# Both norms of an attention and gated feed-forward kernel: ScalarE's reciprocal square root with one Newton step in place of a root and a reciprocal

## The chip, the cores and the metric

The kernel runs on one core of one Trainium2 chip. The metric is the device time of one execution in microseconds (us), given as the median of several runs. The engines are named as in the profile: PE is TensorE (matmuls), PEld its weight loads, DVE is VectorE, ACT is ScalarE, POOL is GpSimd and SP is SyncE, which issues most DMAs.

## The reference

For each of 8 batches there is an attention without a softmax over 8 heads of 64 columns and 576 positions, followed by a root-mean-square norm, and then a gated feed-forward layer whose one half is normalised over its columns and mixed over positions:

```python
kv = np.einsum('bhsd,bhse->bhde', k, v)
out = np.einsum('bhsd,bhde->bhse', q, kv)
rms = np.sqrt(np.mean(out * out, axis=-1, keepdims=True) + 1e-06)
x = out / rms * g_norm                    # per head, then heads side by side: (8, 576, 512)
h = np.maximum(x @ w_in, 0.0)             # d_ff = 1024
u, v = h[..., :512], h[..., 512:]
v_n = (v - mean(v)) / np.sqrt(var(v) + 1e-06)
v_s = np.einsum('ts,bsd->btd', w_spatial, v_n) + b_spatial[None, :, None]
return (u * v_s) @ w_out
```

All is float32. Both norms need 1/sqrt(mean + 1e-6): the first one value for each position and head, the second one value for each position.

## The kernel before

**Tiles.** A batch has 576 positions: four blocks of 128 and a tail of 64. The tails of two batches, an even one and the odd one behind it, are worked on together as a fifth block of 128. The eight heads go as four pairs.

**Attention.** For each pair TensorE makes k'v (L162, tile pskv), ScalarE and VectorE copy the two diagonal blocks to KVB or KVO (L179, L180), and TensorE multiplies by q (L237, pso). The four blocks of 128 positions of a pair stand side by side in one PSUM bank of 512 columns, 8 groups of 64. `norm_a` squares them: either one ScalarE instruction (L223) and a VectorE sum (L224), or eight ScalarE instructions of 64 columns that sum as they go (L220). The sums are ss, 128 x 8. `rsqrt_a` and `rsqrt_b` make 1/sqrt of ss/64 + 1e-6, and `norm_b` multiplies the bank by it (L229, tile x). TensorE transposes x (L265, pstr), and ScalarE and VectorE split the result into a high part XH (L258) and the remainder XL (L259).

**Products in float32.** After the first batch every product of float32 matrices is three passes of the faster format fp32r: high by high, high by low and low by high (`three`, `hl`, `split`; L353 is the high part on ScalarE, L354 the remainder on VectorE). Batch 0 uses plain float32 matmuls while weights are still being decoded and split.

**Feed-forward.** hv (L350, psh) is the half that is normalised: ScalarE empties the bank with a Relu (L323), VectorE makes mean and variance (L329, L330, tile mv), `rsqrt` follows, and the values are normalised either on VectorE (L333) or by one VectorE operation that makes the bias (L336) and one ScalarE instruction (L337). The u half and the mixing over positions are made by a scheme of seven products of half-size blocks instead of eight (L566; banks psua, psub, psuc and psa, psb, psc); VectorE and ScalarE empty and add up their parts (L519 to L549 for U, L615 to L636 and L586, L588 for the gate). In batch 1 u is made without that scheme (`u_unit`, L317 with tile psu, emptied by L453). The last product (L317 with WO) gives the output, which ScalarE copies out (L668). Weights arrive as 64-bit numbers: L713 on ScalarE and L719 to L723 on VectorE decode them; `make_out` does so for the four slabs of w_out, and `split_out` then splits a slab into WO and stores a copy (spare_o, L748). `load_out` loads a slab (L688, tile stage).

**Counts.** There are 40 norms of heads (tile names end in h) and 36 of the feed-forward half (names end in v). The norms of the tails are among both.

**Order.** The text of PLAN, between [ and ], pins the first part of the program (the attention of batch 0 and its first products, some 45 us) for PE, ACT and SP in the order written. FIRST, EVEN, ODD, SEVEN and GATED give the order in which later steps are written down, but there the tile framework's list scheduler (`schedule_with_timeline_sim=True`) puts the instructions of each engine in an order by its own estimate of their times. Each engine then works through its queue in that order and waits at the first instruction that is not ready. All products but the attention's use a pool of four PSUM banks (ps_mm) in turn, so a product starts when the bank of the fourth product before it is empty.

**The lines that the change touches** are `rsqrt_a` and `rsqrt_b`, which both norms call, and the warming instruction L813, whose function decides which table ScalarE loads first.

Of the kernel before, what the change touches and what calls it, by code (L numbers as in the profile page):

```python
# [8 lines left out]
F32 = mybir.dt.float32  # L9
# [3 lines left out]
AF = mybir.ActivationFunctionType  # L13
ALU = mybir.AluOpType
# [5 lines left out]
P = 128  # L20
# [10 lines left out]
EPS = 1e-6  # L31
# [42 lines left out]
def body(ctx: ExitStack, tc, qT, kvm, kvt, g2, w_in, wsT, bsp, w_out, out):  # L74
    nc = tc.nc
# [6 lines left out]
    small = ctx.enter_context(tc.tile_pool(name="small", bufs=2))  # L82
# [46 lines left out]
    epsc = edge.tile([P, 8], F32, name="epsc", tag="epsc")[:, 0:1]  # L129
# [62 lines left out]
    def rsqrt(ss, n, rows, mul, tag):  # L192

        return rsqrt_b(*rsqrt_a(ss, n, rows, mul, tag))

    def rsqrt_a(ss, n, rows, mul, tag):
        a, s0, q, r = (small.tile([P, n], F32, name=f"{x}{tag}", tag=f"{x}{tag}")[0:rows]
                       for x in "asqr")
        nc.scalar.activation(s0, ss, AF.Sqrt, bias=epsc[0:rows], scale=mul)
        nc.vector.tensor_scalar(a, ss, mul, EPS, op0=ALU.mult, op1=ALU.add)  # L200
        nc.vector.reciprocal(q, a)
        return s0, q, r

    def rsqrt_b(s0, q, r):

        nc.vector.tensor_tensor(r, s0, q, op=ALU.mult)
        nc.vector.scalar_tensor_tensor(q, s0, -0.5, r, op0=ALU.mult, op1=ALU.mult)
        nc.vector.scalar_tensor_tensor(r, q, 1.5, r, op0=ALU.add, op1=ALU.mult)
        return r

    def heads(ap):
# [2 lines left out]
    def norm_a(ps, rows=P, accumulate=False):  # L214
        x = work.tile([P, 512], F32, name="x", tag="x")[0:rows]
        ss = small.tile([P, 8], F32, name="ss", tag="ss")[0:rows]
        if accumulate:
            for h in range(8):
                cols = slice(h * D, (h + 1) * D)
                nc.scalar.activation(x[:, cols], ps[0:rows, cols], AF.Square,  # L220
                                     accum_out=ss[:, h:h + 1])
        else:
            nc.scalar.activation(x, ps[0:rows], AF.Square)  # L223
            nc.vector.tensor_reduce(ss, heads(x), axis=AX.X, op=ALU.add)  # L224
        return ps, x, rows, rsqrt_a(ss, 8, rows, 1.0 / D, "h")

    def norm_b(ps, x, rows, parts):
        r = rsqrt_b(*parts)
        nc.vector.tensor_tensor(heads(x), heads(ps[0:rows]),  # L229
                                r.unsqueeze(2).broadcast_to([rows, 8, D]), op=ALU.mult)  # L230
        return x
# [578 lines left out]

    nc.vector.memset(KVB[:, 1], 0.0)
    nc.vector.memset(epsc, EPS)
    nc.scalar.activation(small.tile([P, 1], F32, name="warm", tag="av"), epsc, AF.Sqrt)  # L813
    nc.gpsimd.memset(KVB[:, 0], 0.0)
    for kt in KT:
        nc.gpsimd.memset(kt[TAIL:P], 0.0)
# [223 lines left out]
```

## Time and profile before

| what | value |
|---|---|
| median of 3 runs | 513.03 us (511.57 to 513.43) |
| span of the profiled execution | 511.2 us |
| from the span to the three runs | 0.4 to 2.2 us more |
| PE busy | 498.9 us (98%), 3436 matmuls |
| PE weight loads busy | 438.4 us (86%) |
| DVE busy | 408.8 us (80%), 1193 instructions |
| ACT busy | 292.8 us (57%), 1000 instructions |
| granted TensorE clock | 1.00 |

The profile is of one execution. A row of a group of instructions gives the line, the engine, the operation, what it writes and reads, and how often; busy time is the union of their durations. "A <- B: t" in the list of waits says that A's engine stood idle for t in total until B released it. Times in a timeline count from the start of the span. The device time of the profiled execution itself is not listed; the runs beside it bound it.

### The profile page before, as it was taken

What the parts mean: (1) busy time and instruction counts of PE and PEld (TensorE: products, weight loads), DVE (VectorE), ACT (ScalarE), POOL (GpSimd) and SP (SyncE); (2) the same over time, 40 slices, a digit from 0 to 9 for tenths busy, and PEclk for the clock granted to TensorE, in tenths of its full rate; (3) what the DMA queues carried; (4) which work ended last, traced back from release to release, by engine and by line L of the source; (5) the groups of instructions that cost most, each with busy time, mean ns of one, the idle gap of its engine ahead of it and who ended that gap; (6) DMA issues with size and microseconds to landing.
All of it is one profiled execution on the core that took longest, in us unless ns stands there. A gap on an engine that the chain in (4) does not pass through costs nothing.

```text
span 511.2 us, 9846 instructions
## 1 busy us (share of the span) xinstructions
PE 498.9 (98%) x3436; PEld 438.4 (86%) x3436; DVE 408.8 (80%) x1193; ACT 292.8 (57%) x1000; POOL 28.7 (6%) x58
## 2 busy tenths in 40 slices
PE   6999999999999999999999999999999999999996
PEld 6758788898888899989998899988998889988995
DVE  3898599688997889778795689878898589987870
ACT  2555456896734796456641689347742579536421
POOL 5000000000010300010000100010000100010000
PEclk9999999999999999999999999999999999999999
DMA  7995300635354435354426615324444512315213
GB/s 256 311 347 193 103 23 2 238 90 174 123 193 137 129 126 207 117 170 138 133 93 228 203 41 194 112 78 176 135 165 144 171 30 63 131 42 165 91 76 103
DMA packets 28293, 72.22 MB, mean 141 GB/s; under 512 B 3602, under 2 KB 8210, under 8 KB 26708
## 3 DMA queue, kind: packets, MB, share of 16 engines
q1 hardware_dynamic: 23412, 48.01, 28.6%
q0 software_dynamic: 4832, 23.60, 13.9%
q8 instruction: 27, 0.44, 0.4%
q14 instruction: 22, 0.18, 0.1%
HBM read 58.48 MB, written 13.11 MB: 140 GB/s over the span
## 4 chain that ended last, share of the span: by engine, by line
PE 78%; DVE 8%; ACT 7%; DMA 5%; issue 1%; SPq 0%; ACTq 0%; DVEq 0%
PE pso L317 15%; PE psh L350 12%; PE psb L566 7%; PE pso L237 4%; PE psc L566 4%; PE psa L566 4%; PE psub L566 4%; PE pskv L162 4%; PE psu L428 3%; PE psa L437 3%; PE psua L566 3%; PE psh L404 3%; PE psuc L566 2%; PE pstr L265 2%; DMA KV<-kvm 2%; ACT x L220 2%
## 5 line engine op out<-in xcount | busy, mean ns | idle before, releaser
L317 PE MATMUL pso<-WO,G 128*128 128x512 f32 x384 | 94.4, 397 | 0.0
L317 PEld LDWEIGHTS pso<-WO,G 128*128 128x128 f32 x384 | 70.6, 188 | 14.5
L353 ACT CAST G<-SUMg 128x288 fp32r<-128x288 f32 (+1 forms) x56 | 22.8, 406 | 44.6 <-DVE SUMg L588 44.4
L220 ACT ACTIVATE x<-pso 128x64 f32<-128x64 f32 x208 | 44.8, 254 | 5.7 <-PE pso L237 5.5
L220 ACT ACTIVATION_READ_ACCUMULATOR x<-pso 128x1 f32 x208 | 43.9, 240 | 0.0
L350 PE MATMUL psh<-WVL,XH 128*128 128x512 f32 x112 | 43.9, 392 | 0.0
L350 PE MATMUL psh<-WVH,XH 128*128 128x512 f32 x112 | 43.8, 396 | 0.0
L350 PE MATMUL psh<-WVH,XL 128*128 128x512 f32 x112 | 43.3, 391 | 0.0
L668 ACT COPY o<-pso 128x512 f32<-128x512 f32 x35 | 20.2, 594 | 38.9 <-PE pso L317 28.7
L354 DVE TENSOR_TENSOR VL<-v,VH 128x512 fp32r<-128x512 f32 (+1 forms) x56 | 34.6, 620 | 2.7 <-ACT VH L353 2.2
L353 ACT CAST VH<-v 128x512 fp32r<-128x512 f32 (+1 forms) x56 | 31.7, 574 | 3.3 <-DVE v L382 2.1
L337 ACT ACTIVATE v<-v,mv,rv 128x512 f32<-128x512 f32 x28 | 23.5, 840 | 10.6 <-DVE mv L336 10.5
L354 DVE TENSOR_TENSOR G<-SUMg,G 128x288 fp32r<-128x288 f32 (+1 forms) x56 | 23.4, 417 | 7.2 <-ACT G L353 6.9
L258 ACT ACTIVATE XH<-pstr,gcol 128x512 fp32r<-128x512 f32 x28 | 19.4, 700 | 11.4 <-PE pstr L265 11.2
L566 PE MATMUL psb<-WSH,VH 128*128 128x288 f32 x84 | 25.6, 305 | 0.3 <-DVE U L549 0.2
L329 DVE BATCH_NORM_STATS2 s<-v 128x6 f32<-128x512 f32 x32 | 21.9, 689 | 4.5 <-ACT v L323 3.9
L350 PEld LDWEIGHTS psh<-WVH,XH 128*128 128x128 f32 x112 | 21.0, 188 | 4.6 <-ACT o L668 0.2
L350 PEld LDWEIGHTS psh<-WVL,XH 128*128 128x128 f32 x112 | 21.1, 188 | 4.4
L566 PE MATMUL psb<-WSL,VH 128*128 128x288 f32 x84 | 24.8, 295 | 0.0
L350 PEld LDWEIGHTS psh<-WVH,XL 128*128 128x128 f32 x112 | 21.0, 188 | 4.3
L162 PEld LDWEIGHTS pskv<-KV 128*64 128x64 f32 x512 | 18.1, 140 | 7.8 <-issue 3.9
L566 PE MATMUL psb<-WSH,VL 128*128 128x288 f32 x84 | 24.6, 295 | 0.0
(244 smaller groups left out, 1419.4 us busy)
## 6 DMA issues: line engine op xcount, KB each, us to landing
KV<-kvm SPq DMA_DIRECT2D x31, 512.0 KB, 5.0
WO<-spare_o POOLq DMA_DIRECT2D x12, 1024.0 KB, 7.0
UX<-spare_u POOLq DMA_DIRECT2D x18, 512.0 KB, 5.7
out<-o SPq DMA_DIRECT2D x32, 256.0 KB, 2.6
qt<-qT SPq DMA_DIRECT2D x16, 288.0 KB, 3.5
stage<-w_in SPq DMA_DIRECT2D x8, 512.0 KB, 6.5
qt<-qT SPq DMA_DIRECT2D x16, 256.0 KB, 2.7
KT<-kvt SPq DMA_DIRECT2D x32, 64.0 KB, 4.8
```

Of the source, the lines that this page charges most:

```text
L162: return nc.tensor.matmul(ps[h:h + D, at:at + D], of[:, 0, h:h + D], of[:, 1, h:h + D], start=c == 0, stop=c == NC)
L220: nc.scalar.activation(x[:, cols], ps[0:rows, cols], AF.Square, accum_out=ss[:, h:h + 1])
L237: nc.tensor.matmul(ps[:, c * P:(c + 1) * P], qt[:, c * P:(c + 1) * P], st[p], start=True, stop=True)
L258: nc.scalar.activation(hi, ps, AF.Copy, scale=gcol)
L317: nc.tensor.matmul(ps, lt, rh, start=i == 0, stop=i == n - 1)
L329: nc.vector.bn_stats(s6, v)
L337: nc.scalar.activation(v, v, AF.Identity, bias=m, scale=r)
L350: nc.tensor.matmul(ps, lt, rh, start=k == 0 and i == 0, stop=k == NP - 1 and i == 2)
L353: nc.scalar.copy(hi, x)
L354: nc.vector.tensor_tensor(lo, x, f32(hi), op=ALU.subtract)
L566: nc.tensor.matmul(ps, lt, rh, start=start and i == 0, stop=stop and i == len(pairs) - 1, skip_group_check=True)
L668: nc.scalar.copy(o, ps)
```

## The change

Before, ScalarE makes s0, the square root of a = ss * mul + EPS, while VectorE makes a once more and its reciprocal q. Then r = s0 * q is a first value of 1/sqrt(a), and two more VectorE operations improve it: q = -0.5 * s0 * r, r = (q + 1.5) * r. Now ScalarE makes the first value y of 1/sqrt(a) itself, and three VectorE operations are one Newton step on it: r = -0.5 * mul * y * y, r = (ss + EPS/mul) * r, which is -0.5 * a * y * y, and r = (r + 1.5) * y. The VectorE operations go from five to three for each norm. The sums ss (or the variance in mv) are now read by VectorE behind ScalarE's instruction instead of beside it.

```diff
     def rsqrt_a(ss, n, rows, mul, tag):
-        a, s0, q, r = (small.tile([P, n], F32, name=f"{x}{tag}", tag=f"{x}{tag}")[0:rows]
-                       for x in "asqr")
-        nc.scalar.activation(s0, ss, AF.Sqrt, bias=epsc[0:rows], scale=mul)
-        nc.vector.tensor_scalar(a, ss, mul, EPS, op0=ALU.mult, op1=ALU.add)
-        nc.vector.reciprocal(q, a)
-        return s0, q, r
-
-    def rsqrt_b(s0, q, r):
-
-        nc.vector.tensor_tensor(r, s0, q, op=ALU.mult)
-        nc.vector.scalar_tensor_tensor(q, s0, -0.5, r, op0=ALU.mult, op1=ALU.mult)
-        nc.vector.scalar_tensor_tensor(r, q, 1.5, r, op0=ALU.add, op1=ALU.mult)
+        y, r = (small.tile([P, n], F32, name=f"{x}{tag}", tag=f"{x}{tag}")[0:rows] for x in "yr")
+        nc.scalar.activation(y, ss, AF.Abs_reciprocal_sqrt, bias=epsc[0:rows], scale=mul)
+        return ss, y, r, mul
+
+    def rsqrt_b(ss, y, r, mul):
+
+        nc.vector.scalar_tensor_tensor(r, y, -0.5 * mul, y, op0=ALU.mult, op1=ALU.mult)
+        nc.vector.scalar_tensor_tensor(r, ss, EPS / mul, r, op0=ALU.add, op1=ALU.mult)
+        nc.vector.scalar_tensor_tensor(r, r, 1.5, y, op0=ALU.add, op1=ALU.mult)
         return r
...
-    nc.scalar.activation(small.tile([P, 1], F32, name="warm", tag="av"), epsc, AF.Sqrt)
+    nc.scalar.activation(small.tile([P, 1], F32, name="warm", tag="yv"), epsc, AF.Abs_reciprocal_sqrt)
```

From L209 on every line's number is 3 less in the changed program (L323 becomes L320, L713 becomes L710). ScalarE's order has one load of a function table in either program, ahead of the warming instruction.

The scheduler's order changes too, outside the pinned part. Three places follow. The first is ScalarE's queue behind the pinned part, in batch 1. WTL and WTH are the tail of the mixing weights, v is the Relu that empties psh, G is the gate of batch 0, and t is the first step of the decoding of a slab of w_out. Before:

```order
L787 CAST WTL_88<-WTL_87 64x576
L180 COPY KVB<-pskv 64x2x64
L789 CAST WTL_88<-WTL_87 1x576
L323 ACTIVATE v<-psh 128x512 x2
L789 CAST WTL_88<-WTL_87 1x576
L353 CAST G<-U 128x512
L353 CAST GT<-U 128x64
```

Some rows further down, behind the other three casts of G, the same queue goes on before the change:

```order
L323 ACTIVATE v<-psh 128x512
L220 ACTIVATE x,ss<-pso 128x64 x2
L199 ACTIVATE sv<-mv,epsc 128x1
L713 ACTIVATE t<-stage 128x512
L199 ACTIVATE sv<-mv,epsc 128x1
```

The same place of ScalarE's queue after the change:

```order
L784 CAST WTL_88<-WTL_87 64x576
L180 COPY KVB<-pskv 64x2x64
L786 CAST WTL_88<-WTL_87 1x576
L710 ACTIVATE t<-stage 128x512
L320 ACTIVATE v<-psh 128x512 x2
L786 CAST WTL_88<-WTL_87 1x576
L350 CAST G<-U 128x512
```

The decoding step t stands ahead of the two Relus that empty psh, where it stood behind the third Relu.

The second place is SyncE's queue of DMAs at about the same time. spare_o are the stored copies of split slabs, stage is the load of the next slab, KV and KT are keys and values of a later pair. Before:

```order
L748 DMA spare_o<-WO 128x512 x3
L142 DMA KV_105<-kvm 128x1024
L748 DMA spare_o<-WO 128x512
L688 DMA stage<-w_out 128x1024
L142 DMA KV_104<-kvm 128x1024
```

After the change:

```order
L745 DMA spare_o<-WO 128x512 x4
L685 DMA stage<-w_out 128x1024
L142 DMA KV_105<-kvm 128x1024
L142 DMA KV_104<-kvm 128x1024
L143 DMA KT_106<-kvt 64x256
```

The load of the slab moves ahead of one load of keys and values.

The third place is VectorE's queue in batch 4, where the seven products of u end (300 to 320 us of the span before). U is added up from psub and psuc, v is the normalised half of the tails, SUMg its difference of halves, and names in v and h are norms. Before:

```order
L336 SCALAR_TENSOR_TENSOR mv<-mv,rv 128x1
L538 TENSOR_TENSOR U<-psub,U 128x288
L201 RECIPROCAL qh<-ah 128x8
L206 TENSOR_TENSOR rv<-sv,qv 128x1
L207 SCALAR_TENSOR_TENSOR qv<-sv,rv 128x1
L208 SCALAR_TENSOR_TENSOR rv<-qv,rv 128x1
L333 TENSOR_SCALAR v<-v,mv,rv 128x512
L206 TENSOR_TENSOR rh<-sh,qh 128x8
L529 TENSOR_TENSOR U<-psub,U 128x288
L393 TENSOR_TENSOR SUMg<-v 128x256
L207 SCALAR_TENSOR_TENSOR qh<-sh,rh 128x8
L544 TENSOR_TENSOR U<-psub,U 128x288
```

After the change:

```order
L333 SCALAR_TENSOR_TENSOR mv<-mv,rv 128x1
L535 TENSOR_TENSOR U<-psub,U 128x288
L203 SCALAR_TENSOR_TENSOR rv<-yv 128x1
L204 SCALAR_TENSOR_TENSOR rv<-mv,rv 128x1
L205 SCALAR_TENSOR_TENSOR rv<-rv,yv 128x1
L330 TENSOR_SCALAR v<-v,mv,rv 128x512
L526 TENSOR_TENSOR U<-psub,U 128x288
L203 SCALAR_TENSOR_TENSOR rh<-yh 128x8
L390 TENSOR_TENSOR SUMg<-v 128x256
L541 TENSOR_TENSOR U<-psub,U 128x288
```

The additions to U keep their order, and the operations of the norms between them are fewer.

## The prediction

> **What bounds the kernel now.** I read the page first (busy time of each engine), then a table of stretches, then the list of waits for TensorE, and last the timeline at the places where the new order differs. The page's first part:
>
> ```profile
> PE 498.9 (98%) x3436; PEld 438.4 (86%) x3436; DVE 408.8 (80%) x1193; ACT 292.8 (57%) x1000; POOL 28.7 (6%) x58
> ```
>
> TensorE is busy for 498.9 of 511.2 us. The change takes work from VectorE, which is busy for 80%. So the question is how much TensorE waits for VectorE. The table of stretches (from and to, length, then busy us of PE, PEld, DVE, ACT and POOL with instruction counts, clock, DMA share, GB/s) places TensorE's 12.3 us of idle time:
>
> ```profile
> 0.00:24.00 24.00, 18.87 (x158) 15.76 (x159) 14.07 (x37) 8.89 (x21) 7.43 (x20) 1.00 0.88 281
> 24.00:504.00 480.00, 476.84 (x3267) 420.32 (x3266) 394.28 (x1156) 282.68 (x977) 21.27 (x38) 1.00 0.41 134
> 504.00:512.00 8.00, 3.20 (x14) 2.28 (x13) 0.42 (x1) 1.18 (x3) 0.00 (x0) 0.94 0.49 164
> 88.00:150.00 62.00, 60.67 (x486) 54.10 (x486) 53.61 (x160) 44.92 (x151) 2.68 (x4) 1.00 0.47 157
> 190.00:210.00 20.00, 19.59 (x178) 18.81 (x177) 18.88 (x53) 12.61 (x57) 1.06 (x2) 1.00 0.45 153
> 300.00:320.00 20.00, 19.26 (x146) 18.50 (x146) 19.14 (x63) 18.34 (x94) 1.06 (x2) 1.00 0.48 158
> 420.00:440.00 20.00, 19.60 (x152) 19.16 (x151) 18.73 (x63) 18.15 (x93) 1.06 (x2) 1.00 0.39 132
> 456.00:464.00 8.00, 8.00 (x37) 6.48 (x36) 5.73 (x12) 5.50 (x11) 1.59 (x3) 1.00 0.67 200
> ```
>
> Idle are 5.1 us in the first 24 us (VectorE has 14 of 24 us of work there, the DMA engines are 0.88 busy) and 4.0 us after the last matmul (511.2 - 504 - 3.20), where VectorE has one copy left. Between 24 and 504 only 480 - 476.84 = 3.16 us are idle, and four stretches hold nearly all of it: 1.33, 0.41, 0.74 and 0.40 us. In the last three VectorE is full (18.7 to 19.1 of 20 us). A busy row can hide a little, since a matmul's end is drawn after its successor's start; the weight loads show the same waits longer. TensorE's waits from 24 to 504 us, first as matmuls, then the same as weight loads (total, times, longest):
>
> ```profile
> PE pstr L265 <- DVE x L229: 0.4, 2, 0.3
> ...
> PE psa L566 <- DVE U L549: 0.3, 1, 0.3
> PE psb L566 <- DVE U L549: 0.2, 1, 0.2
> PE psa L566 <- DVE U L544: 0.2, 1, 0.2
> ...
> PEld psb L566 <- DVE U L549: 0.8, 2, 0.5
> PEld psa L566 <- DVE U L549: 0.6, 1, 0.6
> PEld psa L566 <- DVE U L544: 0.5, 1, 0.5
> ```
>
> The three waits for L549 and L544 are 0.7 us as matmuls and 1.9 as loads; the normalised tile (L229) is waited for twice, 0.4 us. I take twice the idle time as the real loss: some 6 us between 24 and 504, of which ScalarE or VectorE decide nearly all. That is the ceiling of what a faster norm can give: 1.2%.
>
> A rule speaks against this reading. The Trainium skill, "Perfetto Trace Analysis", section Identifying the Most-Contended Engine, says that matmul busy time is no good measure of TensorE's headroom and that weight-load busy time and MFU are. By it 14% of the span, some 72 us, would be open. The trace does not agree: in 456 to 464 the loads are busy 6.48 of 8 us (81%) while 37 matmuls follow one another every 0.22 us with no wait; 81% is what a full TensorE looks like with 512 columns.
>
> **The change part by part.** Instructions by line (count, least/median/greatest ns):
>
> ```profile
> L199 ACT ACTIVATE sh<-ss,epsc x40: 287/302/437, 12.9 to 438.3; 128x8 f32<-128x8 f32 x40
> ...
> L200 DVE TENSOR_SCALAR ah<-ss x40: 159/166/173, 12.9 to 439.3; 128x8 f32<-128x8 f32 x40
> L200 DVE TENSOR_SCALAR av<-mv x36: 131/153/155, 43.4 to 476.2; 128x1 f32<-128x1 f32 x36
> L201 DVE RECIPROCAL qh<-ah x40: 191/196/204, 13.1 to 440.1; 128x8 f32<-128x8 f32 x40
> L201 DVE RECIPROCAL qv<-av x36: 109/164/166, 44.9 to 476.4; 128x1 f32<-128x1 f32 x36
> ...
> L208 DVE SCALAR_TENSOR_TENSOR rh<-qh,rh x40: 147/159/170, 14.1 to 441.5; 128x8 f32<-128x8 f32 x40
> ```
>
> From the list of waits, the timeline (start, length) and the chain:
>
> ```profile
> DVE rv L206 <- ACT sv L199: 3.0, 6, 0.6
> ...
> 110.24 0.14 DVE L200 TENSOR_SCALAR av<-mv 128x1 f32<-128x1 f32 x1
> 110.30 0.16 DVE L200 TENSOR_SCALAR ah<-ss 128x8 f32<-128x8 f32 x1
> 110.42 0.17 DVE L201 RECIPROCAL qv<-av 128x1 f32<-128x1 f32 x1
> ...
> 290.39 0.17 DVE av L200
> ...
> 290.84 0.17 DVE rv L206
> ```
>
> Removed are L200 and L201 in 76 norms. At full durations: 40 x (166+196) + 36 x (153+164) ns = 25.9 us. Packed behind other work one costs only the distance to the next start, 0.06 to 0.12 us (110.24, 110.30, 110.42): 152 x 0.09 = 13.7 us. So VectorE loses 14 to 26 us of 408.8. The three operations left are of L208's kind and count; L206 to L208 were three as well, so they cost nothing new. The ScalarE instruction keeps its shape, bias and scale; a different function I price as the same row, 0.29 to 0.44 us, change 0.
>
> Latency gains less. From L200 to L206 it is 0.45 us in the row of 290.39, but the ScalarE root ran beside them for 0.3 us plus two hand-overs, and this stays; a lone norm gets 0.1 us shorter (an estimate: 0.45 less 0.3 and the hand-overs), one that waits for ScalarE (the six waits of 3.0 us) not at all: VectorE then stands at its first operation instead of its third.
>
> A scheduler orders everything outside the hand-written start by its own estimates, so less VectorE work also shuffles the program; the rows in the section on the change show it. Priced by stretch:
>
> - 0 to 24 and after 504: nothing. No norm releases TensorE there.
> - 24 to 88: nothing; TensorE is full.
> - The ends of the first products in batches 2, 4 and 6 (190, 300, 420): idle 0.41 + 0.74 + 0.40 = 1.55, by loads 3.1 us. In the second of them five norms end on VectorE (L208 in that stretch: busy, count):
>
> ```profile
> 300.00:320.00 20.00, 0.80 (x5) 1.00 0.48 158
> ```
>
>   So 10 operations leave, 0.9 us packed and 1.7 at full length, out of the queue that holds the L544 and L549 that TensorE waits for. But ScalarE is as full (18.34, 18.15 of 20), and the hidden half may stay. Ends: 0 and -3.1; I take half, **-1.5**.
> - 88 to 150: here an order change costs. The decode of the third slab of the output weights (L713 on ScalarE) stood behind the four casts of G; now it stands ahead of the two L323 that empty PSUM. Rows of ScalarE, SyncE and TensorE:
>
> ```profile
> 98.18 0.67 ACT L789 CAST WTL<-WTL 1x576 fp32r<-1x576 f32 x1
> 98.87 1.09 ACT L323 ACTIVATE v<-psh 128x512 f32<-128x512 f32 x2
> ...
> 103.36 0.59 ACT L323 ACTIVATE v<-psh 128x512 f32<-128x512 f32 x1
> ...
> 104.42 0.67 ACT L713 ACTIVATE t<-stage 128x512 f32<-128x512 f32 x1
> ...
> 94.46 0.33 SPq L142 DMA_DIRECT2D KV<-kvm  x1
> 94.88 0.39 SPq L748 DMA_DIRECT2D spare_o<-WO  x1
> 95.32 0.42 SPq L688 DMA_DIRECT2D stage<-w_out  x1
> ...
> stage<-w_out SPq DMA_DIRECT2D x4, 512.0 KB, 5.1
> ...
> 100.46 0.38 PE L317 MATMUL psu<-XH,WUH 128*128 128x288 f32 x1
> ...
> 104.00 0.40 PE L317 MATMUL psu<-XH,WUH 128*128 128x288 f32 x1
> ```
>
> ScalarE is free for L713 at 98.85. The load was issued at 95.32, behind a KV load; it moves ahead of that, so at 94.9 to 95.3, and lands 5.1 us later: 100.0 to 100.4. ScalarE stands 1.1 to 1.6 us, then runs L713 for 0.6, and both L323 and all behind them are 1.7 to 2.2 us late. TensorE's next product (100.46) needs the bank that the first L323 frees, and had 1.0 us of room; the third (104.00) had none behind the L323 that ended at 103.95. L713 is no longer in ScalarE's queue after that, which gives 0.6 back: TensorE runs 1.2 to 1.7 us later from about 107 us on. Against it, its later start lets the engines that feed it catch up before the stalls at 128 to 144 (0.9 of the 1.33 us, by loads twice that), and VectorE's relief helps. Ends: -1.8 and +1.7; I take **+0.4**.
>
> Sum: -1.5 + 0.4 = **-1.1 us**. The profiled span is 511.2 us; the three timed runs are 0.4 to 2.2 above it, their median 513.03 by 1.8. A change inside the span carries over one to one: **511.9 us**. On its own, by the ends of the parts that can go together, 510.5 to 513.4.
>
> **The rivals.**
>
> *TensorE's waits go.* If the lighter VectorE lets ScalarE catch up too and the early decode costs nothing, three quarters of the 6 us ceiling come back: -4.4, so 508.6. For it speaks that VectorE is the full engine in three of the four stretches; against it that ScalarE is full beside it in two. The rule of the Trainium skill above points this way, with far more.
>
> *ScalarE stands at the early decode, and nothing is caught up: slower.* Place: the L713 after L789, as priced; it decides if the load lands after about 99.3 us (98.85, plus 1.0 of room, less 0.6). Price +1.7 and no gain elsewhere: 514.6. The fourth slab's L713 also moves up, ahead of the copy of KVB and an XH that TensorE reads; a second stand of 1 us there makes 515.7.
>
> *The shuffle costs elsewhere.* Outside the start nearly every row of VectorE moves; +3 to +5 from a place that I have not found, so 517.
>
> *The function is not in the loaded table.* One load is in the trace:
>
> ```profile
> 0.75 1.28 ACT L813 ACT_TABLE_LOAD   x1 [0.75 <-PEq L1029]
> ```
>
> If each of 76 norms switched there and back, 152 x 1.28 = 195 us of ScalarE work would come on top. The new program's order has a single load at the start, as before, so nearly nothing is left of this. The Trainium skill, "ScalarE: Activation LUTs", section Table sets, warns of this: functions come in sets with one expensive anchor each, and its section What it computes sends an Rsqrt to VectorE's reciprocal with Sqrt, which is the code before. Its load of about 1283 ns agrees with the 1.28 us row.
>
> **How the numbers follow.** Forecast 0.52, waits go 0.20, early decode 0.20, shuffle 0.06, table 0.02. About 0.5% (2.6 us) is what a measurement of this kernel can tell from no change: faster means below 510.5, slower above 515.6. Faster: most of the first rival and the low edge of the forecast, 0.22. Slower: shuffle, table and the double stand, 0.11. The rest, 0.67, is the same. The range runs from 508.8, the middle of the first rival, which leaves out 0.09, to 515.0, above the single stand, which leaves out 0.11.
>
> **What would show it.** Right: VectorE busy 14 to 26 us lower, about 152 instructions fewer and none at the old L200 and L201; one table load; the ScalarE instruction at 0.3 us; TensorE still over 97% busy; its idle time in 190 to 210, 300 to 320 and 420 to 440 below 1.55 together; ScalarE idle for over 1 us before the decode near 99 us, released by the DMA of w_out, and a late first psu behind it. Wrong: TensorE's idle time from 24 to 504 unchanged or above 3.2 us without that stand, or a span below 508, which the waits in this trace cannot pay for.

## The result and the profile after

The changed kernel takes 516.36 us (median of 10 runs, 514.28 to 517.12) against 513.12 us before (10 runs, 511.57 to 514.85): a ratio of 1.0059, 95% interval 1.0042 to 1.0076. It is slower by some 3 us, and above the range of the prediction. The profiled execution took 516.85 us, its span is 515.1 us.

The first part of the page after the change:

```profile
PE 499.9 (97%) x3436; PEld 438.9 (85%) x3436; DVE 392.2 (76%) x1041; ACT 291.2 (57%) x1000; POOL 28.7 (6%) x58
```

VectorE lost 408.8 - 392.2 = 16.6 us and 152 instructions. ScalarE's new function costs what the root cost (median 303 ns for eight values a row, 302 before), and there is one load of a table, as before:

```profile
L198 ACT ACTIVATE yh<-ss,epsc x40: 289/303/436, 12.7 to 442.4; 128x8 f32<-128x8 f32 x40
```

```profile
0.75 1.28 ACT L810 ACT_TABLE_LOAD   x1 [0.75 <-PEq L1026]
```

So the operations did what was foreseen. The table of stretches (columns as before) shows that TensorE's idle time grew all the same. The last three rows are the ends of the first products in batches 2, 4 and 6, some 4 to 5 us later than before:

```profile
0.00:24.00 24.00, 18.43 (x153) 15.37 (x154) 12.61 (x30) 8.88 (x21) 7.40 (x20) 0.86 0.89 283
24.00:504.00 480.00, 474.38 (x3255) 418.04 (x3254) 379.17 (x1011) 279.91 (x974) 21.30 (x38) 1.00 0.41 134
...
130.00:170.00 40.00, 37.15 (x278) 32.08 (x277) 30.05 (x77) 17.70 (x56) 2.68 (x4) 1.00 0.44 145
194.00:214.00 20.00, 19.53 (x176) 18.49 (x175) 18.66 (x49) 12.67 (x58) 1.06 (x2) 1.00 0.50 170
305.00:325.00 20.00, 19.69 (x154) 19.25 (x152) 18.45 (x55) 18.61 (x94) 1.06 (x2) 1.00 0.48 162
424.00:444.00 20.00, 19.80 (x156) 19.56 (x155) 17.91 (x52) 17.73 (x93) 1.06 (x2) 1.00 0.39 133
```

From 24 to 504 us 5.62 us are idle, where it was 3.16; 2.85 of them lie between 130 and 170. The list of waits for TensorE (total, times, longest) names releasers that the list of before did not have, all but the last row, whose counterpart (the normalised tile) cost 0.4 us before as well:

```profile
PE psb L563 <- DVE SUMg L585: 0.9, 1, 0.9
PE psu L314 <- ACT v L320: 0.9, 1, 0.9
PE psa L563 <- ACT o L665: 0.7, 1, 0.7
PE pskv L162 <- DMA KT<-kvt: 0.6, 1, 0.6
PE psa L434 <- DVE U L436: 0.6, 1, 0.6
PE pstr L262 <- DVE x L226: 0.4, 1, 0.4
```

To see where the time went I compare the start of the same matmul in both traces. The changed kernel is 0.60 us late at 37.6 us, at the end of the pinned part (the first matmuls wait for transfers there, and this number changes from one execution to the next; the clock granted in the first 24 us was 0.86 in this execution and 1.00 in that of before), 1.39 at 92, 1.84 at 116, 4.49 at 164 and 3.85 at the last product. So +0.79, +0.45 and +2.65 us are lost at three places, and 0.64 comes back behind them.

**Place A, near 74 us.** VectorE's timeline after the change, and TensorE behind it:

```profile
73.71 0.24 DVE L203 SCALAR_TENSOR_TENSOR rh<-yh 128x8 f32<-128x8 f32 x2
73.88 0.68 DVE L725 TENSOR_TENSOR WVL<-RL,WVH 128x512 fp32r<-128x512 f32 x1
74.59 0.42 DVE L418 TENSOR_TENSOR TA<-SUMg,TA 64x256 fp32r<-64x256 f32 x1
75.04 0.24 DVE L204 SCALAR_TENSOR_TENSOR rh<-ss,rh 128x8 f32<-128x8 f32 x2
75.20 0.45 DVE L436 TENSOR_TENSOR U<-psa,U 128x288 f32<-128x288 f32 x1
...
75.71 1.48 PE L434 MATMUL psa<-stage,V 128*128 128x288 f32 x5 [0.58 <-DVE U L436]
```

The U that empties TensorE's bank stands behind the split WVL and a part of TA, and TensorE waits 0.58 us for it, of the 0.79 lost here. Before, it stood ahead of them:

```profile
73.30 0.23 DVE L206 TENSOR_TENSOR rh<-sh,qh 128x8 f32<-128x8 f32 x2
73.45 0.45 DVE L439 TENSOR_TENSOR U<-psa,U 128x288 f32<-128x288 f32 x1
73.82 0.68 DVE L728 TENSOR_TENSOR WVL<-RL,WVH 128x512 fp32r<-128x512 f32 x1
```

**Place B, near 104 us.** This is the early decode. It hardly waited for its load. The load was issued at 95.39 us and took 4.9 us, so it landed at 100.3; ScalarE had ended the row ahead of t at 100.24, and t starts at 100.35. It is the decode's own 0.68 us that push the Relus back, and TensorE's psu behind the third of them:

```profile
99.57 0.67 ACT L786 CAST WTL<-WTL 1x576 fp32r<-1x576 f32 x1
100.35 0.68 ACT L710 ACTIVATE t<-stage 128x512 f32<-128x512 f32 x1
101.06 1.09 ACT L320 ACTIVATE v<-psh 128x512 f32<-128x512 f32 x2
...
105.54 0.59 ACT L320 ACTIVATE v<-psh 128x512 f32<-128x512 f32 x1
...
stage<-w_out SPq DMA_DIRECT2D x1, 512.0 KB, 4.9
...
106.18 0.40 PE L314 MATMUL psu<-XH,WUH 128*128 128x288 f32 x1 [0.91 <-ACT v L320]
```

**Place C, near 138 us.** w is a pair of tiles that take sums of weights on their way to a stored copy. It shares a ring of two buffers (tag "stg", in work) with o, the output tiles. ScalarE, VectorE and TensorE:

```profile
134.93 0.68 ACT L665 COPY o<-pso 128x512 f32<-128x512 f32 x1
...
139.72 0.42 DVE L351 TENSOR_TENSOR w<-v,w 128x256 fp32r<-128x256 f32 x1 [2.10 <-DMA out<-o]
140.07 0.45 DVE L585 SCALAR_TENSOR_TENSOR SUMg<-U,psa 128x288 f32<-128x288 f32 x1
...
140.57 0.40 PE L563 MATMUL psb<-WSH,VH 128*128 128x288 f32 x1 [0.94 <-DVE SUMg L585]
...
142.00 0.66 PE L262 MATMUL pstr<-ident,x 128*128 128x128 f32 x4 [0.38 <-DVE x L226]
```

VectorE stands 2.10 us at w until the store of an output tile has landed, and the gate's sum, which TensorE waits for, stands behind w. With the waits for the copy o (0.7) and for KT (0.6) of the list above, TensorE's waits here come to 2.6 us; before the change it waited 0.8 us in this stretch, at other places. In that trace the sum (L588) stood 2 us ahead of w, and VectorE did not wait at w at all:

```profile
136.44 0.45 DVE L588 SCALAR_TENSOR_TENSOR SUMg<-U,psa 128x288 f32<-128x288 f32 x1
...
138.43 0.42 DVE L354 TENSOR_TENSOR w<-v,w 128x256 fp32r<-128x256 f32 x1
```

### The profile page after: what moved, and what is told of

Its sections match the earlier page's. It is cut to its first block, busy times and chain, and to the rows that moved or that the text cites. A ratio compares the mean times of both kernels' runs of the same rounds, so it can differ in the third digit from the quotient of the medians.

```text
span 515.1 us, 9633 instructions
## 1 busy us (share of the span) xinstructions
PE 499.9 (97%) x3436; PEld 438.9 (85%) x3436; DVE 392.2 (76%) x1041; ACT 291.2 (57%) x1000; POOL 28.7 (6%) x58
## 4 chain that ended last, share of the span: by engine, by line
PE 83%; DVE 6%; ACT 5%; DMA 4%; issue 0%; SPq 0%; ACTq 0%
PE pso L314 19%; PE psh L347 13%; PE psb L563 6%; PE psub L563 5%; PE pso L234 5%; PE pskv L162 4%; PE psc L563 4%; PE psua L563 3%; PE psu L425 3%; PE psa L563 3%; PE psuc L563 3%; PE psh L401 3%; PE pstr L262 2%; PE psu L314 2%; PE psa L434 2%; PE psh L314 2%
## 5 line engine op out<-in xcount | busy, mean ns | idle before, releaser
L351 DVE TENSOR_TENSOR T<-SUMu,T 128x576 fp32r<-128x576 f32 x12 | 9.1, 756 | 20.6 <-ACT T L350 20.6
```

Of the source, the lines that this page charges most:

```text
L351: nc.vector.tensor_tensor(lo, x, f32(hi), op=ALU.subtract)
```

## The experiments

Theory **order**: the loss comes from where instructions now stand in the queues, at these three places. Rival **operations**: the norms themselves take longer (the new function, or the first VectorE operation that now waits for it). To tell them apart the order has to be fixed by hand. A function called at the end of the body ties each engine's instructions to one another in an order given as a list, one for each engine:

```python
for k in steps:
    if last is not None:
        tc.add_manual_dep(made[k], last.name,
                          mybir.DependencyInfo(mybir.DependencyClass.NoSync,
                                               mybir.DependencyReason.DATA), reason="order")
    last = made[k]
```

Such a tie is of the class NoSync: it fixes the order and asks for no waiting. In e1, e3 and e4 the list stands ahead of the code, so their line numbers are 60 higher than the changed kernel's. The kernel before ran beside each group of experiments, with medians from 512.64 to 512.97 us; each ratio is against those runs.

**e1: the changed arithmetic in the order of before.**

```diff
 (the changed kernel)
+    in_order(nc, tc)      # all engines: the order of before, without L200 and L201
```

> The changed arithmetic (ScalarE's reciprocal root and three VectorE operations), but every engine's queue in the order of the kernel before, without the two removed operations. Theory 'order' (the +3.2 us come from where instructions stand in the queues, the operations themselves cost nothing): 512.0 to 513.3 us, at or just below before. Rival 'operations' (the new function of ScalarE, or the first VectorE operation that now waits for it, makes each norm later): 515.5 to 517, as the changed kernel. VectorE's busy time 16 to 17 us below before in both.

Measured: 512.77 us, ratio to before 0.9999 (0.9977 to 1.0021). In this order the operations cost nothing that can be measured; the rival falls. VectorE is busy for 393.5 us, 15.3 less than before the change.

**e2: the old arithmetic in the changed order.**

```diff
 (the kernel before)
+    in_order(nc, tc)      # all engines: the changed order, L200 and L201 put in
```

> The arithmetic of before (root, reciprocal, five VectorE operations for each norm), but every engine's queue in the order of the changed kernel; the two removed operations stand where the order of before had them, or ahead of the first operation that uses them. Theory 'order': as slow as the changed kernel or slower, 516 to 518.5 us, since VectorE also carries its 152 instructions again. Rival 'operations': 512.5 to 514 us, as before.

Measured: 521.97 us, 1.0171 (1.0144 to 1.0198). Even slower than foreseen: 5.6 us above the changed kernel. Compared at the same matmuls, its trace loses 9.72 us against that of before, 4.51 of them behind 164 us, where the changed kernel gains 0.64. So the changed order has no room for the 152 operations there, or not at the places that I chose for them; this run does not tell which.

**e3 and e4: halves.** The order of before up to 170 us and the changed order behind it, and the reverse:

```diff
 (the changed kernel)
+    in_order(nc, tc)      # first 745 instructions of PE, 330 of DVE, 249 of ACT, 100 of SP: from before
```

> The changed arithmetic; the order of before up to the end of batch 1's gate stage (170 us), the changed order behind it. Theory 'order' says that everything is lost before 170 us and that the changed order behind it gives some 0.5 us back: 511.8 to 513. Rival 'operations': 515.5 to 517. A third case, that the changed order costs behind 170 us as well: 513.5 to 515.

> The changed arithmetic; the changed order up to 170 us, the order of before behind it. Theory 'order': 516 to 517.5 us, all of the loss and none of the small return. Rival 'operations': 515.5 to 517 as well (this run alone doesn't tell the two apart, the run with the halves exchanged does).

Measured: 511.99 us, 0.9984 (0.9970 to 0.9998), with the old order first, and 517.34 us, 1.0090 (1.0059 to 1.0121), with the changed order first. All of the loss is ahead of 170 us. The first of them is the only kernel with the full arithmetic that beats the one before, by 0.65 us, and the interval just leaves out no change.

**e5, e6, e7: the three places, each with the order of before.** All else is the changed kernel.

```diff
 (the changed kernel)
+    in_order(nc, tc)      # A: first 400 of PE, 175 of DVE, 125 of ACT, 55 of SP from before
+    in_order(nc, tc)      # B: DVE 175 to 206, ACT 125 to 149, SP 55 to 60 from before
+    in_order(nc, tc)      # C: PE 400 to 744, DVE 207 to 329, ACT 150 to 248, SP 61 to 99 from before
```

> The changed kernel with its own order, except that up to 97 us every queue has the order of before (it undoes the place near 74 us where VectorE makes norms and splits ahead of the U that TensorE waits for). In the traces TensorE loses some 0.7 us there. Theory 'three places, each for itself': 515.5 to 516 us. Rival 'one chain' (an early delay sets off the later ones): below 515. Rival 'soaked up' (later waits take in what is lost early): no change, 516 to 517.

> The changed kernel with its own order, except between 97 and 111 us, where the queues have the order of before: the decode of the third slab behind the Relus that empty psh, its load behind the load of keys and values. The place that the prediction priced at +1.2 to +1.7 before the catching up; in the traces TensorE is 0.5 to 0.8 us later behind it. Theory 'each for itself': 515.5 to 516. Rival 'one chain': below 515. Rival 'soaked up', as the prediction had it: 516 to 517.

> The changed kernel with its own order, except between 111 and 170 us, where the queues have the order of before: the gate stage of batch 1, where TensorE loses 2.7 us in the traces. Theory 'each for itself': 513.4 to 514.2. Rival 'one chain' (that stage is late only because TensorE comes to it late): 515 to 516.5. Rival 'soaked up': 512.5 to 513.3, since the rest would be taken in.

Measured: A mended 515.95 us, 1.0052 (1.0034 to 1.0070); B mended 515.73, 1.0050 (1.0031 to 1.0068); C mended 513.09, 1.0003 (0.9990 to 1.0015). C holds 0.0056 of the 0.0059. The time is below what 'each for itself' had foreseen (513.4 to 514.2), and inside the range of its rival 'soaked up'. The trace of this kernel decides (table below): A and B still cost 0.80 and 0.34 us in it, but the stretch of C is 0.66 us shorter than before the change, and the later batches 0.68. A and B alone are within the uncertainty of a comparison, but the traces show them each time.

**e8: w alone.** On VectorE's queue near 138 us, in the changed order (- and +):

```diff
-L351 w<-v,w
 L585 SUMg<-U,psa
 L204 rh, L205 rh
-L476 v<-WUH,WUL
 L205 rh
 L226 x<-pso,rh
 L633 SUMu<-psb,SUMp
 L351 G<-SUMg,G
+L351 w<-v,w
+L476 v<-WUH,WUL
```

> The changed kernel with its own order and two instructions moved on VectorE, near 138 us: the tile w, which waits for the DMA that stores an output tile of the same ring of two buffers, and the sum of weights after it stand behind the gate's sum, x and G instead of ahead of them. In the trace VectorE stands 2.1 us at w, and TensorE 0.9 and 0.4 us behind it, with a transfer of keys delayed as well. If w is what costs in this stage: 513.7 to 515.2. If the loss there is spread over the order (output copies late on ScalarE, w only one of several): 515.5 to 516.4.

Measured: 514.67 us, 1.0025 (1.0011 to 1.0040). Two instructions moved give back 0.0034 of the 0.0059, 1.7 us; the rest of C, 0.0022 against the 1.0003 above, is not theirs. VectorE's wait at w is nearly gone; from its list of waits:

```profile
DVE w L351 <- DMA out<-o: 0.2, 1, 0.2
```

The other kernels with the changed order there wait for different times. The same row in e4 (changed order up to 170 us), in e5 (A mended) and in e6 (B mended):

```profile
DVE w L411 <- DMA out<-o: 0.4, 1, 0.4
```

```profile
DVE w L351 <- DMA out<-o: 2.6, 1, 2.6
```

```profile
DVE w L351 <- DMA out<-o: 1.8, 1, 1.8
```

By the same matmuls as above (us gained or lost in each stretch against the trace of before; one execution each):

| stretch | changed | e1 | e3 | e4 | e5 | e6 | e7 | e8 | e9 | e10 |
|---|---|---|---|---|---|---|---|---|---|---|
| to 38 | 0.60 | 0.38 | 0.17 | -0.20 | 0.37 | 0.05 | 0.94 | -0.69 | 0.39 | 0.38 |
| 38 to 92 (A) | 0.79 | -0.04 | -0.02 | 0.81 | 0.00 | 0.78 | 0.80 | 0.78 | 0.01 | 0.77 |
| 92 to 116 (B) | 0.45 | -0.01 | 0.01 | 0.37 | 0.39 | -0.02 | 0.34 | 0.39 | -0.02 | 0.35 |
| 116 to 164 (C) | 2.65 | -0.17 | -0.52 | 0.62 | 3.54 | 2.11 | -0.66 | 0.47 | 0.94 | 0.82 |
| 164 to the end | -0.64 | -0.14 | -0.69 | -0.28 | -0.49 | -0.56 | -0.68 | -0.64 | -0.65 | -0.67 |
| wait at w | 2.1 | - | - | 0.4 | 2.6 | 1.8 | 0 | 0.2 | 0.1 | 0 |

A and B cost the same in every kernel that has the changed order there, and nothing in the others: each for itself, neither one chain nor soaked up. Where w stands ahead of the gate's sum, C follows the wait at w: 0.4, 1.8, 2.1 and 2.6 us of wait, 0.62, 2.11, 2.65 and 3.54 us lost. The wait varies because the store of the same output tile lands 2.4 to 4.6 us after the copy that fills it has ended; the kernel with 0.4 us was profiled in the fastest of its eight runs.

**e9 and e10: all three mended, and one more move at C.**

```diff
 (the changed kernel)
+    in_order(nc, tc)      # A and B as above, w and L476 behind G
```

> The changed kernel with its own order, and the three places mended together: the order of before up to 111 us, and w and the sum of weights behind the gate's sum near 138 us; all else as in the changed kernel. Theory 'each for itself': the loss is 0.75 near 74 us, 0.45 near 104, and at w what it waits for; so 512.9 to 513.8 us, between before and the kernel with w alone moved (1.0025). Rival 'one chain': no better than w alone, 514.2 to 515.

```diff
 ACT, with w and L476 behind G on DVE
 L217 x<-pso (seven), L665 o<-pso (third)
+L665 o<-pso (fourth)
 L217 x<-pso, L255 XH<-pstr, L220 x<-pst
-L665 o<-pso (fourth)
```

> The changed kernel with its own order, w and the sum of weights behind the gate's sum as before, and one more move: on ScalarE the copy of the fourth output tile (it waits behind one accumulation, an XH and a square of a norm) stands right behind the third output copy. It frees the bank that TensorE waits 0.70 us for. If what is left of the loss in this stage is that wait: 0.5 to 0.8 us less than with w alone, 513.6 to 514.3. If the XH and the square, now 0.5 us later, take its place: 514.5 to 515, as with w alone.

Measured: 513.47 us, 1.0005 (0.9991 to 1.0019), for the three places: the sum of the parts, as the theory says. The move of the output copy gave nothing: 514.79 us, 1.0033 (1.0016 to 1.0049). The 0.7 us for that copy went, and another wait stands in e10, put down to the sums of weights (v):

```profile
PE pskv L162 <- DVE v L380: 0.6, 1, 0.6
```

That wait is in e9 too (0.7 us), without the move of the copy, and not in e8. So what is left of the loss at C, some 0.5 to 0.9 us, I have not pinned to one instruction.

**e11 and e12: how much VectorE's load is worth in the order of before.** Without the Newton step (r is ScalarE's first value; this leaves out that part of the computation), and with the two removed operations done twice:

```diff
 (the changed kernel, order of before)
-        nc.vector.scalar_tensor_tensor(r, y, -0.5 * mul, y, op0=ALU.mult, op1=ALU.mult)
-        nc.vector.scalar_tensor_tensor(r, ss, EPS / mul, r, op0=ALU.add, op1=ALU.mult)
-        nc.vector.scalar_tensor_tensor(r, r, 1.5, y, op0=ALU.add, op1=ALU.mult)
-        return r
+        return y
```

> The changed kernel without the Newton step: the first value of ScalarE is taken as it is, so VectorE has no operation at all for the root of a norm (another 228 instructions fewer, some 25 us); the order is that of the kernel before. It measures what a lighter VectorE can give at most. Theory of the prediction (TensorE's waits of some 6 us are decided by VectorE and ScalarE, so less work on VectorE takes them down): 508.6 to 511. Rival 'the order decides, not the load': 512 to 513, as with the Newton step in that order.

```diff
 (the kernel before, order of before)
-        nc.vector.tensor_scalar(a, ss, mul, EPS, op0=ALU.mult, op1=ALU.add)
-        nc.vector.reciprocal(q, a)
+        for _ in range(2):
+            nc.vector.tensor_scalar(a, ss, mul, EPS, op0=ALU.mult, op1=ALU.add)
+        for _ in range(2):
+            nc.vector.reciprocal(q, a)
```

> The kernel before, in its own order, with the two operations that the change removes done twice in each norm: 152 more VectorE instructions, 14 to 26 us more. Theory 'in a given order VectorE has room': 512.5 to 513.5, no change. Rival 'VectorE is at its limit where TensorE waits': 514.5 to 518.

Measured: 510.98 us, 0.9958 (0.9942 to 0.9975), without the step, and 520.40 us, 1.0142 (1.0111 to 1.0173), with the doubled operations. The two pages' first lines:

```profile
PE 497.9 (98%) x3436; PEld 438.0 (86%) x3436; DVE 369.4 (73%) x813; ACT 293.0 (58%) x1000; POOL 28.6 (6%) x58
```

```profile
PE 502.9 (97%) x3436; PEld 439.1 (85%) x3436; DVE 429.5 (83%) x1345; ACT 292.4 (56%) x1000; POOL 28.7 (6%) x58
```

The first lies at the upper edge of the range of the prediction's theory, and its rival falls; the second is above both ranges, so that VectorE has no room for more. In one and the same order 152 instructions more cost 7.5 us, 152 fewer give nothing (the first kernel), and 380 fewer give 2.0 us: the kernel before sits at the bend of that curve. This is not VectorE's load alone, since each added operation also stands ahead of its own norm's result. With the doubled operations TensorE waits 2.2 us for normalised tiles, against 0.4 before:

```profile
PE pstr L267 <- DVE x L231: 1.3, 3, 0.8
PE pst L190 <- DVE x L231: 0.9, 1, 0.9
```

What is load and what is a later norm these runs do not separate.

**e13 to e16: who moved the order.** Here the scheduler makes the order itself, and the removed operations come back as dead work in all norms, in the feed-forward norms, or in the head norms:

```diff
 (the changed kernel; the condition is True, tag == "v" or tag == "h")
         nc.scalar.activation(y, ss, AF.Abs_reciprocal_sqrt, bias=epsc[0:rows], scale=mul)
+        if tag == "v":
+            a, q = (small.tile([P, n], F32, name=f"{x}{tag}", tag=f"{x}{tag}")[0:rows] for x in "aq")
+            nc.vector.tensor_scalar(a, ss, mul, EPS, op0=ALU.mult, op1=ALU.add)
+            nc.vector.reciprocal(q, a)
```

> The changed arithmetic, and in every norm the two removed operations once more as dead work whose result nobody reads; the scheduler makes the order itself. VectorE's load is that of before, only the function of ScalarE and what is read by whom is changed. Theory 'lean norms moved the order': its order is near that of before, so 512.5 to 514.5. Rival 'a draw' (any change of the program draws an order of its own, worth some us either way): anywhere from 511 to 522.

> The changed kernel, where only the 40 norms of heads are lean; the 36 of the feed-forward half carry the two removed operations as dead work (72 instructions); the scheduler makes the order itself, and that is nearly the order of the changed kernel (99% of it). Theory 'order': the places near 74, 104 and 138 us cost as in the changed kernel, and the 72 instructions cost on top: 516 to 519. Rival 'load' (what the changed order lost is the room that VectorE has): the same place on that scale as the share of the work removed, 512.5 to 514.5.

> The changed kernel, where only the 36 norms of the feed-forward half are lean; the 40 of heads carry the two removed operations as dead work (80 instructions); the scheduler makes the order itself, nearer to that of before on TensorE and ScalarE (86 and 85%) than to the changed one (69 and 75%). Theory 'lean head norms moved the order': 512.5 to 514.5, as before. Rival 'a draw': anywhere from 511 to 522.

The last kernel leaves the Newton step out and has the scheduler's own order:

```diff
 (the changed kernel, own order)
-        nc.vector.scalar_tensor_tensor(r, y, -0.5 * mul, y, op0=ALU.mult, op1=ALU.mult)
-        nc.vector.scalar_tensor_tensor(r, ss, EPS / mul, r, op0=ALU.add, op1=ALU.mult)
-        nc.vector.scalar_tensor_tensor(r, r, 1.5, y, op0=ALU.add, op1=ALU.mult)
-        return r
+        return y
```

> The changed kernel without the Newton step, with the order that the scheduler makes for it. In the order of before this load gave 510.98 us, 0.9958 of before. Theory 'each order has its price beside the load': 511 to 516. Rival 'the scheduler's order is worth more than an old one when the load falls this far': below 510.5.

Measured: dead work in all norms 515.17 us, 1.0039 (1.0019 to 1.0059); in the feed-forward norms 517.22, 1.0075 (1.0051 to 1.0100); in the head norms 516.51, 1.0060 (1.0037 to 1.0083); without the Newton step 512.92, 0.9997 (0.9978 to 1.0016). The theory that the lean head norms moved the order to its harm falls: with VectorE's load of before (406.0 us busy) the scheduler still made an order that is 2 us slower, and with the head norms' load back one that is 3.5 us slower. The theory 'order' for the dead work in the feed-forward norms (516 to 519) holds, its rival 'load' falls. None of the five orders that the scheduler made for these variants of the new arithmetic (with the changed kernel's own) is as good as the order of before; without the Newton step too, the order of before gives 510.98 and its own order 512.92, so that the last rival (below 510.5) falls. The rival 'a draw' allowed any time that could have come, so that these runs do not show it.

A wait at w alone is not what costs. Without the Newton step, in the scheduler's order, VectorE stands 2.93 us at w, and the profile lists no wait of TensorE between 128 and 139 us:

```profile
131.23 0.42 DVE L348 TENSOR_TENSOR w<-v,w 128x256 fp32r<-128x256 f32 x1 [2.93 <-DMA out<-o]
```

It costs where something that TensorE needs soon stands behind it. One thing is common to the three kernels with dead work: the wait at A. In e13, with the dead work in all norms (line numbers 4 higher):

```profile
PE psa L438 <- DVE U L440: 0.6, 1, 0.6
```

It is in the other two as well, and all three lose 0.77 or 0.78 us between 38 and 92, so at A the lighter load is not needed. I did not try what in the new arithmetic makes it; that stays open, as does why the scheduler's estimate puts w ahead of the gate's sum.

## Why the prediction was wrong

By its terms: it added up 0 up to 88 us, +0.4 from 88 to 150 and -1.5 behind that, -1.1 in all. The traces have +0.60 up to 38 us (which varies), +0.79 up to 92, +3.10 up to 164 and -0.64 behind that, +3.85 in all.

- *TensorE is the bound, and 6 us are the ceiling.* The bound was right. What the norm's root can give in the order of before is less: with no VectorE operation left in it, 2.0 us came back. The rule of the Trainium skill ("Perfetto Trace Analysis", Identifying the Most-Contended Engine), by which 72 us would be open, does not agree with this: there too TensorE's loads are busy for 86%.
- *VectorE loses 14 to 26 us; the function costs the same; one table load.* Right: 16.6 us, 303 ns against 302, one load. The Trainium skill's warning ("ScalarE: Activation LUTs", Table sets) that functions lie in different tables does no harm here: the kernel uses the one load of 1.28 us.
- *The ends of the first products in batches 2, 4 and 6: -1.5.* **Failed.** In the order of before the relief is worth 0.1 us: TensorE's idle time in the three stretches goes from 1.55 to 1.48 us. The second of them, with the changed arithmetic in the order of before:

```profile
300.00:320.00 20.00, 19.27 (x147) 18.57 (x146) 18.61 (x53) 18.46 (x94) 1.07 (x2) 1.00 0.48 157
```

  VectorE's queue up to the L544 and L549 that TensorE waits for, before the change:

```profile
306.65 0.17 DVE L200 TENSOR_SCALAR ah<-ss 128x8 f32<-128x8 f32 x1
306.77 0.69 DVE L229 TENSOR_TENSOR x<-pso,rh 128x512 f32<-128x512 f32 x1
307.38 0.19 DVE L201 RECIPROCAL qh<-ah 128x8 f32<-128x8 f32 x1
307.60 0.69 DVE L401 TENSOR_TENSOR TA<-v,TA 64x512 fp32r<-64x512 f32 x1
...
312.01 0.46 DVE L544 TENSOR_TENSOR U<-psub,U 128x288 f32<-128x288 f32 x1
...
313.82 0.45 DVE L549 TENSOR_TENSOR U<-psuc,U 128x288 f32<-128x288 f32 x1
```

  The same in the changed arithmetic with the order of before:

```profile
304.25 0.16 DVE L263 SCALAR_TENSOR_TENSOR rv<-yv 128x1 f32<-128x1 f32 x1 [0.30 <-ACT yv L258]
...
306.89 0.69 DVE L286 TENSOR_TENSOR x<-pso,rh 128x512 f32<-128x512 f32 x1
307.61 0.69 DVE L458 TENSOR_TENSOR TA<-v,TA 64x512 fp32r<-64x512 f32 x1
...
312.02 0.46 DVE L601 TENSOR_TENSOR U<-psub,U 128x288 f32<-128x288 f32 x1
...
313.83 0.45 DVE L606 TENSOR_TENSOR U<-psuc,U 128x288 f32<-128x288 f32 x1
```

  From the L200 at 306.65, or the x at 306.89, to the additions VectorE works without a pause in both traces, and of the ten removed operations only two, L200 and L201 above, stand in that piece of the queue. Without L201 the way from x to TA takes 0.72 us in place of 0.83. Leaving out L200 saves nothing: x starts 0.2 us behind the norm's last operation either way. Ahead of it, at 304.25 us, VectorE now stands 0.30 us until ScalarE's y is there, so what is saved earlier is lost in that wait. That execution was 0.1 us late at this point and came out of the stretch level with the one before: that is the relief. The ten were counted in a stretch of 20 us and not in the queue ahead of the additions. In the changed order the three stretches together idle 0.98 us (0.47 + 0.31 + 0.20), below the 1.55 that was named as a sign, and behind 164 us the kernel gains 0.64, less than half of the term: near 200 us it loses a further 0.4, in batch 4 it gains 0.8.
- *24 to 88: nothing, TensorE is full.* **Failed**, by 0.79 us at A. A full engine is full because the others serve it in time; a new order can end that.
- *The early decode.* The place and the direction were right, and it does cost; the way was not. The load landed at 100.3 us, inside the forecast 100.0 to 100.4, but ScalarE came to t only at 100.24 and not at 98.85, since all was 1.39 us late by then; so it stood 0.1 us and not 1.1 to 1.6, and the decode's own 0.68 us did it. With A mended ScalarE came at 99.21, and there the load took 4.2 us and landed at 99.24: that it never stood for long is in part luck. TensorE was 0.79 us later at 104 (2.18 - 1.39) and 0.45 at 116, against 1.2 to 1.7.
- *Its later start lets the feeding engines catch up before the stalls at 128 to 144.* **This is the step that failed most.** It was argued from the stalls of the old order. In the new order there is a stall of another kind at that place, w ahead of the gate's sum, and the stretch lost 2.65 us more. The term of +0.4 measured +3.10. Undoing the order there alone brings the kernel back to 1.0003. The sign named for being wrong is what came: TensorE idle for more than 3.2 us (5.62) without a stand at the decode.
- *The rival "the shuffle costs elsewhere, 517".* This is what happened, with a chance of 0.06 given to it. The place could have been found beforehand: in VectorE's new order an instruction that needs a buffer from a DMA stands ahead of one that TensorE waits for. The prediction priced ScalarE's and SyncE's new order, and VectorE's only as less work.
- *Sums.* Three are slightly off, and none changes the account: the weight loads' idle time in the three stretches is 1.19 + 1.50 + 0.84 = 3.5 us by its rows, not 3.1; three quarters of 6 us are 4.5, not 4.4; and 513.03 + 1.7 is 514.7, not 514.6.

## What to carry to other kernels

Where a list scheduler makes the order, a change of the instructions is also a new order, and at a bound engine that is 97% busy the order can be worth more than the instructions: here 0 for the instructions and 3 us for the order. Fix the old order by hand to measure the two apart, and keep it if it wins. Before forecasting, search each engine's new queue for an instruction that waits for a DMA or a ring buffer and that has moved ahead of one that the bound engine waits for. Here moving one such instruction, and one behind it, gave back over half of the loss.

## What the runs showed of the hardware

- The store of a 256 KB output tile released its buffer 2.4 to 4.6 us after the copy into it had ended, for the same instruction at nearly the same place of the program (the kernel with the changed order up to 170 us: copy ended 134.69, w started 137.05; the one with A mended: 134.52 and 139.09). In the traces a longer wait at w went with a longer loss at C. The kernel with the changed order up to 170 us ran 514.29 to 521.48 us; that this spread comes from the store is not shown, as only its fastest run was profiled.
- The start of the program varies too: at the same matmul near 38 us the traces of kernels with one and the same pinned part differ by 1.6 us (-0.69 to 0.94 against before). The clock granted in the first 24 us differs as well: where it was 0.86 (the changed kernel and four of the experiments) that matmul was 0.49 to 0.94 us late, where it was 1.00, from 0.20 early to 0.39 late, and where it was 0.93, from 0.69 early to 0.37 late. So the clock can be part of it, and is not all.
